# A Fourier mixing and low-rank MLP kernel: batch 1 folded at the output with even and odd products, channel steps of batches 1 and 2 given out by need, one of the first narrow sums on GpSimd

## The chip, the cores and the metric

The kernel runs on one NeuronCore of a Trainium2 chip. The engines are named as in the profile: PE (TensorE, matmuls; PEld are its weight loads), DVE (VectorE), ACT (ScalarE), POOL (GpSimd) and SP (SyncE, which issues DMAs). The metric is the device time of one execution in microseconds. Lower is better.

## The reference

```
X  = fft(fft(x, axis=1), axis=2).real          # x: 8 x 3136 x 256, f32
h  = (X^T @ U @ V)^T                           # U: 3136 x 32, V: 32 x 3136, per batch
u  = X + h
out = u + relu(u @ w_ch1) @ w_ch2              # w_ch1: 256 x 1024, w_ch2: 1024 x 256
```

The real part of a two-dimensional transform of real data is a sum of products with cosine and sine tables: along the sequence (3136 points) and along the channels (256 points). The rest is a low-rank token mixer and a two-layer MLP over channels with a residual.

## The kernel before

All 8 x 3136 rows are cut into 49 chunks of 512 rows. The main loop runs over chunks `c` and, in each, over eight hidden tiles `j`. At each `j` it does `first_product(c, j)` (two matmuls of 512 columns, line 735, and a ReLU on ACT, line 737). At each odd `j` it does `second_product(c - 1, j // 2)` (eight matmuls of 256 columns, line 751); every second one of these is closed by three sums on DVE into the output tile (lines 757, 759, 760). At `j == 3` it calls `front(c + 1)`, which makes the next chunk's input u: two low-rank matmuls (line 709) and sums with the transformed data on DVE (line 725, one for each half of the channels, S and T). The tile u is also transposed by DMA for the output sums.

Between these, the loop runs small steps from a table `due`, keyed by 8 x c + j. They prepare the later batches, b = 1 to 7 (batch 0 is done ahead of the loop; b counts from 0, so "second batch" is b = 1). For each batch there are:

- `fold(b)`: 16 steps that fold x along channels and sequence on DVE (`along_d`, line 386; `mirror`, line 395; `half`, line 399), with the loads of the next batch among them, issued by POOL.
- `seq(b, par, typ, pn)`: the sequence transform, eight steps. A pair of steps gives the products of the even and of the odd tiles (line 485, four matmuls of 425 columns each), which DVE sums into the tiles A and B (lines 500, 504). From batch 2 on the first of a pair is split further into narrower matmuls (`quarters`, line 446); `halves` (line 430) is a form with two groups of 229 columns, used in batch 1 for one of the two types.
- the channel transform. Batches 0 and 1 use `chan`: for each of four column ranges and each half h two matmuls (lines 631, 633) and a copy. From batch 2 on `even_ch` and `odd_ch` use half the matmuls (lines 643, 652): the even product is copied by ACT (line 645), and DVE forms its sum and difference with the odd one (line 654). `across` copies rows of A into the low-rank operand on ACT (lines 664, 666), so that the missing term comes out of the low-rank product.
- `narrow`: channel 0 needs a product of its own, with one row (batches 0 and 1) or six rows (batches 2 to 7 together, `column_steps`), and narrow sums (lines 570 to 574), on DVE for batch 0 and on POOL for the others.
- `joined(b)` (line 468, POOL) joins the sums for U, and from batch 2 on it also sends the first-channel row by DMA on SP's queue (line 673). `lowrank(b)` (line 678) makes the low-rank operand TA (line 680, ACT), which `front` reads.

The order up to chunk 1 is written out by hand. From there a planner orders each engine's instructions, with program order as priority: an instruction that it takes for ready may pass one that it takes for blocked. The fold's instructions are pinned behind what stands ahead of them on their engine. PSUM is shared: three buffers ("dft") for the products of all these steps, three for the first product, two for the second.

For batch b the low-rank step is due at about `hi`:

```
hi = 8 * (b * S // CH - 1) + 2        # 42, 90, 138, 186, 234, 282, 330 for b = 1 to 7
```

## Time and profile before

| what | value |
|---|---|
| median of three runs | 447.18 us (447.13 to 447.69) |
| the profiled execution | 447.31 us |
| its span | 445.2 us |
| granted TensorE clock | 1.00 throughout |
| DVE busy | 353.1 us, 79% |
| ACT busy | 297.5 us, 67% |
| POOL busy | 85.7 us, 19% |

The columns of a row of the profile's timeline are: start and length in us, engine, source line, operation, output <- inputs, shapes, how many were merged, and, in brackets, the idle time before it with what ended it. In the groups the mean is in ns. A matmul's end is modelled and overlaps the next matmul, so the cost of a matmul is read from the start of its neighbour. DVE instructions overlap a little too.

### The profile page before, as it was taken

What the parts mean: (1) busy time and instruction counts of PE and PEld (TensorE: products, weight loads), DVE (VectorE), ACT (ScalarE), POOL (GpSimd) and SP (SyncE); (2) the same over time, 40 slices, a digit from 0 to 9 for tenths busy, and PEclk for the clock granted to TensorE, in tenths of its full rate; (3) what the DMA queues carried; (4) which work ended last, traced back from release to release, by engine and by line L of the source; (5) the groups of instructions that cost most, each with busy time, mean ns of one, the idle gap of its engine ahead of it and who ended that gap; (6) DMA issues with size and microseconds to landing.
All of it is one profiled execution on the core that took longest, in us unless ns stands there. A gap on an engine that the chain in (4) does not pass through costs nothing.

```text
span 445.2 us, 8087 instructions
## 1 busy us (share of the span) xinstructions
PE 435.7 (98%) x2960; PEld 316.4 (71%) x3012; DVE 353.1 (79%) x838; ACT 297.5 (67%) x564; POOL 85.7 (19%) x144
## 2 busy tenths in 40 slices
PE   8999999999999999999999999999999999999997
PEld 6456766776677777777777777777777777777775
DVE  8879998888998799878998789878998776443433
ACT  8857747565885669655875569655876569656562
POOL 8973217300931002300211001300000000000000
PEclk9999999999999999999999999999999999999999
DMA  7998997995199437674779537782333332434343
GB/s 133 210 230 180 229 173 117 245 153 103 49 230 265 120 106 216 190 171 73 157 203 222 108 103 216 196 167 71 95 119 95 91 100 73 117 97 121 93 125 112
DMA packets 103249, 65.36 MB, mean 147 GB/s; under 512 B 73806, under 2 KB 99624, under 8 KB 100464
## 3 DMA queue, kind: packets, MB, share of 16 engines
q1 hardware_dynamic: 97528, 39.10, 40.1%
q0 software_dynamic: 5664, 25.75, 21.6%
q8 instruction: 23, 0.38, 0.3%
q14 instruction: 16, 0.13, 0.1%
q10 hardware_dynamic: 18, 0.00, 0.0%
HBM read 29.33 MB, written 25.69 MB: 124 GB/s over the span
## 4 chain that ended last, share of the span: by engine, by line
PE 91%; DVE 2%; DMA 2%; issue 1%; POOL 1%; ACT 1%; DVEq 0%; POOLq 0%
PE p L751 38%; PE p L735 35%; PE pt L485 6%; PE ph L709 5%; DMA xb<-in_x_dram,xidx 2%; PE ptq L446 2%; PE pst L643 1%; PE pst L652 1%; PE m L850 1%; PE ptc L556 1%; ACT h L737 0%; DVE eor L386 0%; PE pst L631 0%; DVE eof L386 0%; PE pst L633 0%
## 5 line engine op out<-in xcount | busy, mean ns | idle before, releaser
L737 ACT ACTIVATE h<-p 128x512 bf16<-128x512 f32 x392 | 222.0, 597 | 119.5 <-PE p L735 107.3
L735 PE MATMUL p<-u,w 128*128 128x512 bf16 x735 | 209.3, 379 | 1.2 <-DVE B L500 0.2
L751 PE MATMUL p<-w,h 128*128 128x256 bf16 x1568 | 203.0, 273 | 1.4
L751 PEld LDWEIGHTS <-h 128*128 128x128 bf16 x1568 | 153.2, 98 | 50.4 <-DVE o L760 0.3
L735 PEld LDWEIGHTS <-w 128*128 128x128 bf16 x784 | 106.1, 144 | 35.1 <-issue 2.0
L757 DVE TENSOR_TENSOR o<-p,ut 128x4 f32<-128x4 f32 (+1 forms) x100 | 16.2, 162 | 54.9 <-PE p L751 53.3
L759 DVE TENSOR_TENSOR o<-p,ut 128x254 f32<-128x254 f32 (+1 forms) x100 | 40.5, 405 | 0.0
L760 DVE TENSOR_TENSOR o<-p,ut 128x254 f32<-128x254 f32 (+1 forms) x100 | 40.5, 405 | 0.0
L468 POOL TENSOR_TENSOR tab<-tf 128x64 bf16<-128x64 f32 x7 | 3.1, 440 | 179.2 <-DVE tf L492 179.1
L386 DVE TENSOR_TENSOR eof<-xf 99x1024 bf16<-99x1024 f32 x28 | 35.8, 1293 | 0.0
L386 DVE TENSOR_TENSOR eor<-xr 99x1024 bf16<-99x1024 f32 x28 | 34.8, 1247 | 0.0
L725 DVE TENSOR_TENSOR u<-ph,S 128x512 bf16<-128x512 f32 (+23 forms) x63 | 34.3, 553 | 0.0
L725 DVE TENSOR_TENSOR u<-ph,T 128x512 bf16<-128x512 f32 (+23 forms) x63 | 34.2, 553 | 0.0
L55 POOL DMA_INDIRECT xf<-in_x_dram,xidx x14 | 17.3, 1234 | 62.0 <-DVE eof L386 48.5
L709 PE MATMUL ph<-va,ta 128*128 128x512 bf16 (+15 forms) x124 | 28.6, 328 | 0.3
L485 PEld LDWEIGHTS <-g 98*128 98x128 bf16 (+1 forms) x152 | 14.7, 98 | 13.1 <-issue 0.7
L395 DVE TENSOR_TENSOR eos<-eof,eor 99x1024 bf16<-99x1024 bf16 (+1 forms) x28 | 19.2, 702 | 0.0
L654 DVE TENSOR_TENSOR S<-evd,pst 128x392 bf16<-128x392 f32 (+1 forms) x24 | 13.5, 564 | 6.4 <-PE pst L652 4.1
L485 PE MATMUL pt<-tabs,g 98*128 98x425 bf16 x80 | 17.6, 344 | 0.0
L457 DVE TENSOR_TENSOR ev<-ptq,ex 128x131 f32<-128x131 f32 (+1 forms) x24 | 6.9, 289 | 12.9 <-ACT ex L450 12.9
L399 DVE TENSOR_TENSOR g<-eos 99x2048 bf16<-99x2048 bf16 (+1 forms) x14 | 16.9, 1217 | 0.0
L485 PE MATMUL pt<-tabc,g 98*128 98x425 bf16 x72 | 15.5, 344 | 0.0
(198 smaller groups left out, 381.0 us busy)
## 6 DMA issues: line engine op xcount, KB each, us to landing
out_dram<-o SPq DMA_DIRECT2D x48, 512.0 KB
xr<-in_x_dram POOLq DMA_DIRECT2D x14, 784.0 KB, 8.2
xb<-in_x_dram POOLq DMA_DIRECT2D x2, 392.0 KB, 7.9
ut<-u SPq DMA_TRANSPOSE x49
w<-in_moe_w_ch_dram POOLq DMA_DIRECT2D x1, 512.0 KB
out_dram<-o SPq DMA_DIRECT2D x4, 128.0 KB
va<-in_moe_V_dram POOLq DMA_DIRECT2D x2, 196.0 KB
w<-in_moe_w_ch_dram POOLq DMA_DIRECT2D x1, 256.0 KB, 7.2
```

Of the source, the lines that this page charges most:

```text
L55: nc.gpsimd.indirect_dma_start(out_, None, bass.AP(t.tensor, t.offset, [[w, rows], [1, w]]), bass.IndirectOffsetOnAxis(idx, 0), element_of ...
L386: pin(nc.vector.tensor_tensor(dst[:, a, :, part * P:(part + 1) * P].rearrange("p i (k t) -> p i k t", k=2), lo, hi, op=AL.subtract if part ...
L395: pin(nc.vector.tensor_tensor(EOS[:, a, :, cols], EOF_[:, a, :, cols], EOR_[:, a, ::-1][:, :, cols], op=op))
L399: pin(nc.vector.tensor_tensor(G[b % 2][par][:, :, cols], EOS[:, 0, :, cols], EOS[:, 1, :, cols], op=AL.add if par == 0 else AL.subtract))
L485: nc.tensor.matmul(pt[:], g[:kp(i), i, P * typ:P * (typ + 1)], tabs[typ][:kp(i), i, par, :], start=(n == 0), stop=(n == NI // 2 - 1))
L709: nc.tensor.matmul(ph, TA[b % 2][:k, s * P:(s + 1) * P], VA[b % 2][:k, lo:hi], start=start, stop=True)
L725: nc.vector.tensor_tensor(u[:, s, col:col + hi - lo], ph[:, col:col + hi - lo], src, op=AL.add)
L735: nc.tensor.matmul(p1[:], W1[:, s, j::JT], k["u"][:, s, :], start=(s == 0), stop=(s == 1))
L737: LAST[0] = nc.scalar.activation(k["h"][:, j, :], p1[:], AF.Relu)
L751: nc.tensor.matmul(p2[:, t % w, :], h[:, j, rs], W2[:, j, :], start=(j == 0), stop=(j == JT - 1))
L759: nc.vector.tensor_tensor(o[:, ts, 1:P], p2[:, :w, 1:P], ut[:, ts, 1:P], op=AL.add)
L760: nc.vector.tensor_tensor(o[:, ts, P + 1:D], p2[:, :w, P + 1:D], ut[:, tT, P - 1:0:-1], op=AL.add)
```

## The change

1. Batch 1's sequence step uses the split form `halves` for both types, where it used it for one.
2. Batch 1's channel step is `even_ch`, `odd_ch` and `across`, as in the later batches, in place of `chan` with two matmuls for each half. Its low-rank product then reads all 128 rows of the operand, and the separate `last_row` sums of batch 1 are gone.
3. `transform` is cut into `sequence` and `channels`, and each gets its own due times. Channels of batches 1 and 2 come at -4, -3, -2, -1, +3, +5, +8, +11 around `hi`, those of the later batches from -12 to -1. `joined`, the row's DMA (`row_in`) and `lowrank` have due times of their own. The folds of batches 1 and 2 move, the column sums of batches 2 to 7 end five steps earlier, and the column loads are 1.86 steps apart in place of 2.
4. Of the two pairs of narrow sums of batch 0, one goes to POOL. The rows for it are copied to one partition by ACT. `ta_rows(1)` moves ahead of that sum's second half.
5. Batch 1's narrow sums have tiles of their own (`tc1`, `tr1`) and run ahead of the sequence steps.

```diff
-        if pn == 0 and (b >= B0 or b == 1 and typ == 1):
+        if pn == 0 and b:
             (quarters if b >= B0 else halves)(d, g, par, typ)
...
+            if single:
+                odd = t["ev"] = wp.tile([P, QW], FP32, tag="ev", name="evc", bufs=4)
+                nc.scalar.copy(odd[3 * R:3 * R + 1], pt[R:R + 1])
+                t["eo"] = gen.tile([KP, 2, QW], FP32, tag="pho", name="eo")[:1]
+                nc.scalar.copy(t["eo"][:, 0], pt[:1])
+                return
...
+            eng = nc.vector if single and par else nc.gpsimd
+            if single and par == 0:
+                nc.scalar.copy(t["eo"][:, 1], t["pt"][2 * R:2 * R + 1])
+                e, o = t["eo"][:, 0], t["eo"][:, 1]
...
     def joined(b):
         join_t(nc.gpsimd)
-        if b >= B0:
-            nc.gpsimd.tensor_copy(TS[:1, 0], trow[:, (b - B0) * R:(b - B0 + 1) * R])
-            nc.sync.dma_start(out=VA[b % 2][R:R + 1, :], in_=rows[b - B0:b - B0 + 1, :])
+        nc.gpsimd.tensor_copy(TS[:1, 0], trow[:, (b - B0) * R:(b - B0 + 1) * R] if b >= B0
+                              else tr1[:])
+    def row_in(b):
+        nc.sync.dma_start(out=VA[b % 2][R:R + 1, :], in_=rows[b - B0:b - B0 + 1, :])
...
-        k = P if b >= B0 else 2 * R + 1
+        k = P if b else 2 * R + 1
...
-        if b < B0:
-            row = list(first_channel(b, eng=nc.gpsimd))
-            yield from row[:2]
-            yield lambda: (row[2](), joined(b))
-            for ch in range(4):
-                for h in range(2):
-                    yield lambda ch=ch, h=h: chan(b, ch * 392 + (1 if ch else 0),
-                                                  (ch + 1) * 392 + 1, h)
-            yield from row[3:]
-            yield lambda: (lowrank(b), last_row(b))
-            return
+    def channels(b):
         for ch in range(4):
             yield lambda ch=ch: (even_ch(b, ch), across(b, ch, False))
-            yield lambda ch=ch: (odd_ch(b, ch), across(b, ch, True), ch < 3 or joined(b))
-        yield lambda: lowrank(b)
+            yield lambda ch=ch: (odd_ch(b, ch), across(b, ch, True))
...
     narrow_0[0]()
+    narrow_0[2]()
     seq(0, 0, 1, 0)
-    for step in narrow_0[1:3]:
-        step()
+    narrow_0[1]()
+    ta_rows(1)
+    late[1]()
...
-    for step in piece(1, 0) + piece(1, 1, tag=("p2", 2)) + late[2:] + late[:2]:
+    for step in piece(1, 0) + piece(1, 1, tag=("p2", 2)) + late[2:] + late[:1]:
...
         if b == 1:
-            spread(list(fold(b)), 4, 23)
-            spread(list(transform(b)), 23, hi)
+            spread(list(fold(b)), 2, 21)
+            row = list(first_channel(b))
+            spread(row[:1], 21, 22)
+            spread(row[1:], 22, 24)
+            spread(list(sequence(b)), 23, hi - 4)
+        elif b == B0:
+            spread(list(fold(b)), hi - 60, hi - 23)
+            spread(list(sequence(b)), hi - 21, hi - 4)
         else:
             spread(list(fold(b)), hi - 66, hi - 35)
-            spread(list(transform(b)), hi - 33, hi)
+            spread(list(sequence(b)), hi - 33, hi - 13)
         if b == B0:
-            for at, step in zip((24, 23, 21, 20, 19, 18, 12), column_steps()):
+            for at, step in zip((24, 23, 21, 20, 19, 18, 17), column_steps()):
                 due.setdefault(hi - at, []).append(step)
+        due.setdefault(hi - (3 if b <= B0 else 11), []).append(lambda b=b: joined(b))
+        if b >= B0:
+            due.setdefault(hi - 10, []).append(lambda b=b: row_in(b))
+        due.setdefault(hi, []).append(lambda b=b: lowrank(b))
+        at = (-4, -3, -2, -1, 3, 5, 8, 11) if b <= B0 else (-12, -10, -8, -6, -4, -3, -2, -1)
+        for n, step in zip(at, channels(b)):
+            due.setdefault(hi + n, []).append(step)
     for n, step in enumerate(column_loads()):
-        due.setdefault(8 + 2 * n, []).append(step)
+        due.setdefault(8 + 52 * n // 28, []).append(step)
```

More of the change, by code (lines that the diff above doesn't have):

```diff
@@ L517 @@
     trow = cpool.tile([1, NB * R], BF16, name="trow")
+    tc1 = cpool.tile([1, 2, R], FP32, name="tc1")
+    tr1 = cpool.tile([1, R], BF16, name="tr1")
     def column_zeros():
@@ L543, in column_loads, with narrow @@
                     yield load
-    def narrow(nb, stationary, dst, tc_, total, tag=("dft", 3), late=None, eng=None):
+    def narrow(nb, stationary, dst, tc_, total, tag=("dft", 3), single=False, late=None):
         t = {}
-        eng = eng or nc.vector
         def products():
@@ L768, in second_product, with sequence @@
             del CK[c]
-    def transform(b):
+    def sequence(b):
         for par in range(2):
@@ L798, in odd_row @@
     def odd_row(i):
-        pho = gen.tile([KP, 2, NQ], I32, tag="pho", name="pho")
-        phase(pho[:], krow[:KP], ncol[:KP, i:i + 1], 15)
-        sine(tabs[0][:, i, :, :NQ], pho[:], 15, 1)
+        pho = gen.tile([KP, 2, QW], I32, tag="pho", name="pho")[:, :, :NQ]
+        phase(pho, krow[:KP], ncol[:KP, i:i + 1], 15)
+        sine(tabs[0][:, i, :, :NQ], pho, 15, 1)
     odd_row(0)
```

19 lines of the change are left out of this document (9 added, 10 removed).

## The prediction

> **What bounds the kernel now.** I read four views in this order: the busy times on the page, a table of busy time by stage, the timeline of one engine at a time around the places where a chunk of 512 rows begins, and the groups of instructions for prices. A step below is one hidden tile j of one chunk (step = 8·chunk + j), as the kernel's own due times count.
>
> ```profile
> PE 435.7 (98%) x2960; PEld 316.4 (71%) x3012; DVE 353.1 (79%) x838; ACT 297.5 (67%) x564; POOL 85.7 (19%) x144
> ```
>
> ```profile
> 36.00:66.00 30.00, 29.83 (x197) 21.08 (x199) 29.80 (x54) 19.63 (x37) 8.40 (x12) 1.00 0.88 192
> 66.00:76.00 10.00, 9.64 (x68) 6.06 (x68) 8.87 (x16) 7.38 (x16) 6.84 (x8) 1.00 0.75 132
> ...
> 107.00:136.00 29.00, 28.36 (x203) 20.46 (x205) 27.48 (x58) 22.93 (x45) 16.07 (x18) 1.00 0.58 135
> ```
>
> The columns after the length are PE, weight loads, DVE, ACT, POOL, granted clock and DMA. PE idles 445.2 - 435.7 = 9.5 us in the whole span, and in the three stages that the change rearranges only 0.17, 0.36 and 0.64 us. So the time is PE's work plus few stalls. The second engine matters as much: DVE is full from 36 to 66 us (29.80 of 30) and nearly so from 107 to 136. Work that moves from PE to DVE is free only where DVE's queue is not already what a matmul waits for.
>
> **The terms.** Prices of what PE loses, from starts of neighbours, because modelled ends overlap:
>
> ```profile
> 54.62 0.56 PE L430 MATMUL pth<-tabc,g 98*128 98x229 bf16 x4
> 55.02 0.88 PE L485 MATMUL pt<-tabc,g 98*128 98x425 bf16 x4
> 55.74 0.89 PE L485 MATMUL pt<-tabs,g 98*128 98x425 bf16 x4
> ...
> 68.15 0.33 PE L631 MATMUL pst<-A,mc 128*128 128x393 bf16 x1
> ...
> 68.49 0.59 PE L735 MATMUL p<-u,w 128*128 128x512 bf16 x2
> ```
>
> (a) *Second batch, fewer matmuls.* Two more of its sequence products take the split form: four narrow matmuls in 0.40 us (54.62 to 55.02) in place of four wide ones in 0.72 (55.02 to 55.74), 2 x 0.32 = 0.64 us. Its channel step did eight pairs of matmuls at 0.34 us (68.15 to 68.49); the even and odd form does eight single ones, which leaves out 8 x 0.167 = 1.34 us. Together **-1.98 us**, all on PE. Nothing is added on PE: the low-rank product contracts 128 rows in place of 65, but its matmuls of 512 columns start the next one after the same time.
>
> (b) *The first narrow sums, and the fold that begins two steps earlier.* On DVE one of the two pairs of sums goes to POOL, with two more one-row copies on ACT. Where this stage ends is here:
>
> ```profile
> 32.75 1.22 DVE L574 TENSOR_TENSOR va<-evc,ptc 1x392 bf16<-1x392 f32 x2
> 34.09 0.57 DVE L635 CAST T<-pst 128x392 bf16<-128x392 f32 x1
> 34.69 0.69 DVE L725 TENSOR_TENSOR u<-ph,S 128x512 bf16<-128x512 f32 x1
> 35.30 0.68 DVE L725 TENSOR_TENSOR u<-ph,T 128x512 bf16<-128x512 f32 x1
> 35.90 2.35 DVE L386 TENSOR_TENSOR eor<-xr 99x1024 bf16<-99x1024 f32 x2
> ```
>
> ```profile
> 34.46 2.36 PE L735 MATMUL p<-u,w 128*128 128x512 bf16 x10
> ```
>
> Chunk 1's input u is whole at 35.98. A product of 512 columns follows the next after 0.22 us (the row of two at 68.49 takes 0.59, one of three below 0.81), so PE has done the eight matmuls left of chunk 0 at 34.46 + 8 x 0.22 = 36.2 and asks for u: 0.2 us to spare. The change puts the first two folds of batch 1 (together that 2.35) at steps 2 and 3, in program order ahead of the copy at 34.09 and of u. DVE saves one sum there (half of 1.22) and the pause before 34.09 (0.12), so u comes some 2.3 - 0.7 = 1.6 us later. Against that stand the 0.2 to spare, one channel pair that PE can do first (0.34), and that the first half of each product needs only the S half of u, which lands 0.6 us before the T half. I take **+0.6**, between 0 (the planner finds other work) and 1.4. POOL's sums I put at nothing: POOL starts them when ACT has copied the row, and what covers them is the rest of batch 0's sequence on PE; they would show as a wait of the first low-rank products.
>
> DVE's prices for the next parts, from starts of neighbours where there are any:
>
> ```profile
> 45.84 1.23 DVE L386 TENSOR_TENSOR eor<-xr 99x1024 bf16<-99x1024 f32 x1
> 46.98 1.22 DVE L386 TENSOR_TENSOR eof<-xf 99x1024 bf16<-99x1024 f32 x1
> ...
> 56.26 0.35 DVE L436 TENSOR_TENSOR ev<-pth,ev 128x196 f32<-128x196 f32 x1
> ...
> 57.15 0.19 DVE L492 TENSOR_TENSOR tf<-pt,ev 128x32 f32<-128x32 f32 x1
> ...
> 94.73 0.30 DVE L457 TENSOR_TENSOR ev<-ptq,ex 128x131 f32<-128x131 f32 x1 [1.44 <-ACT ex L450]
> ...
> 97.22 0.14 DVE L757 TENSOR_TENSOR o<-p,ut 128x4 f32<-128x4 f32 x1
> ```
>
> ```profile
> L395 DVE TENSOR_TENSOR eos<-eof,eor 99x1024 bf16<-99x1024 bf16 x26 | 17.9, 703 | 0.0
> L399 DVE TENSOR_TENSOR g<-eos 99x2048 bf16<-99x2048 bf16 x12 | 14.6, 1214 | 0.0
> ```
>
> ```profile
> 122.22 0.56 DVE L654 TENSOR_TENSOR S<-evd,pst 128x392 bf16<-128x392 f32 x1
> ...
> 123.16 0.15 DVE L757 TENSOR_TENSOR o<-p,ut 128x4 f32<-128x4 f32 x1
> ...
> 123.89 0.68 DVE L395 TENSOR_TENSOR eos<-eof,eor 99x1024 bf16<-99x1024 bf16 x1
> ```
>
> (c) *Batch 1 is spread out.* Its sequence went into steps 23 to 30, on top of the fold of batch 2 at 24 to 55; now it has 23 to 38, the fold 30 to 67, and its channels 38 to 53. The idle PE time there is the 0.17 + 0.36 above. I take **-0.4** of it, ends 0 and -0.5. DVE gains work here: four odd steps of two sums (0.94 us a pair, 122.22 to 123.16) and two more split products (0.89, 56.26 to 57.15), less one row of sums: at most 4 x 0.94 + 2 x 0.89 = 5.5 us. What hides it is that the fold's tail and batch 2's sequence have left these steps. ACT loses eight copies and gets four, with eight half-height ones, in a stage where it is 65% busy (19.63 of 30).
>
> (d) *Batch 2 is pushed together.* Before, its sequence ran at 57 to 70 and its channels at 72 to 86; now 69 to 83 and 86 to 101, beside the fold of batch 3 at 72 to 101, which stays.
>
> A fold is 8 x 1.14 + 4 x 0.70 + 2 x 1.21 = 14.3 us over 31 steps, 0.46 a step. A sequence is 4 x 2.49 (94.73 to 97.22) = 10.0 us over 17 steps, 0.59. Output and input sums are 2 x 0.73 (123.16 to 123.89) + 2 x 0.61 (34.69 to 35.30) = 2.7 us a chunk, 0.33 a step. From step 72 to 85 that is 1.38 us of DVE a step. PE's chunk is 16 + 2 matmuls of 0.22 and 32 of 0.108 (rows of eight and of twelve below: 0.43 for four), 7.4 us, 0.92 a step, and for the sequence 4 x (0.32 + 0.72) / 17 = 0.25: 1.17. DVE falls behind by 0.21 x 14 = 2.9 us. In the same steps before, its load was 0.33 + 0.46 + 4 x 0.94 / 14 = 1.06 against 1.02, 0.5 us. So DVE is some **2.4 us later** than now when chunks 11 and 12 ask for u. How late it is now:
>
> ```profile
> 119.80 1.04 PE L751 MATMUL p<-w,h 128*128 128x256 bf16 x8
> 120.67 0.82 PE L735 MATMUL p<-u,w 128*128 128x512 bf16 x2
> ```
>
> ```profile
> 120.39 0.68 DVE L725 TENSOR_TENSOR u<-ph,S 128x512 bf16<-128x512 f32 x1
> ...
> 135.77 0.54 DVE L725 TENSOR_TENSOR u<-ph,T 128x384 bf16<-128x384 f32 x1
> ```
>
> ```profile
> 136.56 0.81 PE L735 MATMUL p<-u,w 128*128 128x512 bf16 x3
> ```
>
> Chunk 10's u ends at 121.07, after its first product began at 120.67 (two matmuls took 0.82, elsewhere 0.59): late already. Chunk 12's ends 136.31, 0.25 us before use. With 2.4 us more, u misses by 2.1. The cover is PE's own order, which a planner sets from what it expects to be ready:
>
> ```profile
> 63.21 1.47 PE L751 MATMUL p<-w,h 128*128 128x256 bf16 x12
> ```
>
> Twelve second-product matmuls in a row, where eight is a unit: it moves some ahead when u is late. A chunk has 16 of them ready (1.74 us) at that moment, if buffers are free. So 0.4 us of 2.1 is left, and the stalls from DVE's slowing beside POOL (next) stay. I take **+0.5**, ends -0.6 (the idle there now goes) and +2.1 (nothing is moved ahead). If the cover goes, the next thing late is output sums, then PSUM.
>
> ```profile
> 117.89 1.97 DVE L386 TENSOR_TENSOR eor<-xr 99x1024 bf16<-99x1024 f32 x1
> ```
>
> This fold took 1.97 us in place of 1.23, while POOL did the column sums; the PSUM-fed pair at 122.22 held its 0.56. The Trainium skill, *SBUF — State Buffer*, "Who interferes with whom", says that a VectorE instruction with two SBUF inputs and a GpSimd instruction that reads SBUF shut each other out. The trace agrees (1.97 against 1.23). By that rule POOL's late first sum could hold back the early fold of (b) by up to 0.7 us more, and the sum would be -0.5 in place of -1.2; without it it stays -1.2.
>
> (e) *Batches 3 to 7.* Same work, but the four odd steps come at -10, -6, -3 and -1 before the batch's low-rank step, where they were at -16, -12, -8 and -4: one more pair (0.94 us) just ahead of the next input sum.
>
> ```profile
> 185.69 0.48 DVE L725 TENSOR_TENSOR u<-ph,T 128x320 bf16<-128x320 f32 x1
> ```
>
> ```profile
> 186.60 0.59 PE L735 MATMUL p<-u,w 128*128 128x512 bf16 x2
> ```
>
> u of chunk 18 ends at 186.17, 0.43 us before use; 0.94 later it is 0.5 late, in batches 3 to 6 (behind batch 7 no fold follows). Eight second-product matmuls cover that. I take **+0.1**, ends 0 and 4 x 0.5 = 2.0. The low-rank product goes from two steps ahead to the step itself:
>
> ```profile
> 229.58 0.27 PE L678 MATMUL ptt<-mc,tab 128*128 128x256 bf16 x1
> 230.22 0.35 ACT L680 CAST ta<-ptt 32x256 bf16<-32x256 f32 x1
> ...
> 232.73 0.49 PE L709 MATMUL ph<-va,ta 128*128 128x256 bf16 x3
> ```
>
> Its result is on chip at 230.57, 0.99 us after the matmul's start, and is read 3.15 after it; two steps less (1.85) leave 1.3. It stays covered, by 0.3; taken as 0.
>
> (f) *Queues.* On POOL the join of the sums now stands ahead of the next load of x from batch 3 on; it waits for DVE's last sum at the end of the sequence, four steps or more earlier, and the load has a fold's length to land. On SP the first-channel row is now sent at step 80 of batch 2, and waits for this copy:
>
> ```profile
> 118.84 2.37 POOL L610 COPY rows<-rows 6x1567 bf16<-6x1567 bf16 x1
> ```
>
> It ends at 121.2, and step 80 was 120.67. So SP stands for about half a us; behind it are input transposes that are read a chunk (7.4 us) later. The column loads are only drawn together (28 in 52 steps in place of 56). I put (f) at 0.
>
> **The sum.** -1.98 + 0.6 - 0.4 + 0.5 + 0.1 = -1.2 us. The profiled run took 447.31 us, 2.1 more than its span of 445.2; the sum gives 446.1 for it. Its time is 0.13 above the median of the three runs (447.18), so I predict **446.0 us**, 0.27% less. A change under 0.2% (0.9 us) is about what a measurement of this kernel cannot tell from none.
>
> **Rivals.** *All cover holds.* Spreading batch 1 takes its 0.5 of idle, the planner hides the late u of chunk 1, and the idle 0.6 of stage (d) goes too: -1.98 - 0.5 - 0.6 = -3.1, 444.1 us. For it: DVE's queue is shorter in 36 to 76 us. Against it: the early folds are written by hand ahead of chunk 1's u.
>
> *VectorE's queue becomes the bound (slower).* One mechanism: the input sum u stands in DVE's order behind folds and sequence work, and PE waits at the chunk's first product. Price: 2.1 in (d) in place of my 0.5, and 2.0 in (e) in place of 0.1: -1.2 + 1.6 + 1.9 = +2.3, 449.5 us. For it: chunk 10 is already late at 120.67, and DVE is full. Against it: the run of twelve at 63.21, with DVE full for 30 us and PE idle 0.17. It decides when less than about half of that lateness is filled: from 2.1 us of stalls beyond my terms on the kernel is slower.
>
> *Only the first chunk fails.* u of chunk 1 costs its full 1.4 and stage (d) 1.0: -1.98 + 1.4 - 0.4 + 1.0 + 0.1 = +0.1, 447.3 us, no change.
>
> *The removed matmuls were not the bound (it does not do what it says).* If PE had spare time, 1.98 us less of it would come back as waiting, 447.2 us. Against it: PE idles 0.17 of 30 us in the very stage where most of it goes, and its matmuls follow each other at 0.108 and 0.22 us. The Trainium skill, *Perfetto Trace Analysis*, "Identifying the Most-Contended Engine", warns that matmul busy time is a poor measure and names the busy share of weight loads: here 71%, which would speak for this rival. The start-to-start times do not bear that out, so I leave it a small chance.
>
> **How the numbers follow.** Forecast 0.50, with a range of its own of 445.0 to 446.6 (0.44 of it faster by over 0.2%, 0.06 within), all cover holds 0.12, first chunk fails 0.06, not the bound 0.08, VectorE's queue 0.24. Faster 0.44 + 0.12 = 0.56, same 0.06 + 0.06 + 0.08 = 0.20, slower 0.24. The ends of the terms add up to -3.1 and to +3.5 (1.4 + 0 + 2.1 + 2.0 - 1.98); the range for 8 in 10 goes to the fast case, 444.0, and to the slow one, 449.5.
>
> **What would show each step.** (a) Eight matmuls at the channel line of batch 1, none of the full pairs, and split products only for batch 1; PE busy lower by about 2 us. (b) u of chunk 1 near 37.5 in place of 35.98, and PE's first product of chunk 1 then, with a channel pair ahead of it. (c) PE idle from 52 to 72 us under 0.3, DVE below full there. (d) DVE without a pause from step 72 to beyond 90, u of chunks 11 to 13 ending at or after the first product, and long runs of second-product matmuls; stalls over 2 us there make the forecast wrong to the slow side. (e) 0.3 us or more of PE idle behind each batch's low-rank step would be the same fault, repeated. (f) SP's wait for the row under 1 us. Wrong to the fast side: no stall at 36 us.

## The result and the profile after

The changed kernel takes **453.01 us** (median of four, 452.79 to 453.18), beside 447.15 for the kernel before on the same chip: a ratio of 1.0129, 95% interval 1.0112 to 1.0147. It is 5.9 us slower. Forecast were 446.0 us, range 444.0 to 449.5, so the prediction was wrong in sign and size. In the changed kernel the first product is line 750, the second 766, u 740, the low-rank products 724, the operand's matmul and copy 693 and 695, the channel steps 655 to 678, the ReLU 752.

The busy times of the changed kernel's page, and its table by stage with the columns that the prediction's table has (span 451.1 us):

```profile
PE 439.0 (97%) x3004; PEld 317.6 (70%) x3004; DVE 351.9 (78%) x846; ACT 300.0 (67%) x570; POOL 84.6 (19%) x148
```

```profile
36.00:66.00 30.00, 28.96 (x201) 20.15 (x201) 26.88 (x52) 19.99 (x38) 13.02 (x19) 1.00 0.88 181
66.00:76.00 10.00, 10.00 (x69) 7.22 (x67) 9.97 (x23) 6.24 (x12) 3.29 (x5) 1.00 0.65 143
...
107.00:136.00 29.00, 27.12 (x190) 19.44 (x184) 27.88 (x60) 18.11 (x36) 12.88 (x16) 1.00 0.53 142
```

PE now idles 451.1 - 439.0 = 12.1 us where it idled 9.5. In the three stages of the prediction's table it is 1.04, 0 and 1.88 (before 0.17, 0.36 and 0.64). The busy time of PE has risen although matmuls were taken out, for two reasons that have nothing to do with work. The record of the kernel before lacks 52 of its matmuls (2960, with 3012 weight loads), nearly all of the first product, and the changed kernel's lacks none (3004 of each, eight fewer). Each one that is missing leaves a small hole that reads as idle time: of two kernels below with the same time (the join ahead of the mirror copies, and then the mirror copies late), the one with 52 missing reads 434.2 us busy and the complete one 436.4. So some 2 us of the 9.5, here and in the prediction, are no idle time. And where matmuls no longer follow one another, each modelled end adds to the busy time, so waits have to be read from starts. Three places stand out.

First, the low-rank products, once per batch. These are PE's rows with a wait at line 724 of the changed kernel, for batches 3 to 7, each from the timeline around that batch; the last bracket is the idle time before the row:

```profile
185.19 0.53 PE L724 MATMUL ph<-va,ta 128*128 128x320 bf16 x3 [0.58 <-issue]
...
236.21 0.50 PE L724 MATMUL ph<-va,ta 128*128 128x256 bf16 x3 [0.54 <-issue]
...
287.21 0.48 PE L724 MATMUL ph<-va,ta 128*128 128x192 bf16 x3 [0.53 <-issue]
...
337.93 0.45 PE L724 MATMUL ph<-va,ta 128*128 128x128 bf16 x3 [0.49 <-ACT ta L695]
...
388.64 0.42 PE L724 MATMUL ph<-va,ta 128*128 128x64 bf16 x3 [0.46 <-ACT ta L695]
```

Together 2.60 us. The matmul before each of them is counted to its modelled end, 0.16 us beyond its pitch, so from start to start it is about 5 x 0.16 = 0.8 more, 3.4 us. Batch 1 has the same wait once (79.66 us, 0.63). What the product waits for stands in ScalarE's timeline of batch 3; the operand's second matmul started at 182.95:

```profile
182.61 0.53 ACT L678 COPY va<-A 64x392 bf16<-64x392 bf16 x1
183.15 0.60 ACT L752 ACTIVATE h<-p 128x512 bf16<-128x512 f32 x1
183.76 0.51 ACT L676 COPY va<-A 64x391 bf16<-64x391 bf16 x1
184.29 0.60 ACT L752 ACTIVATE h<-p 128x512 bf16<-128x512 f32 x1
184.79 0.35 ACT L695 CAST ta<-ptt 32x256 bf16<-32x256 f32 x1
```

ScalarE has no pause. The copy of 0.35 us that makes the operand stands behind two channel copies and two ReLUs and starts 1.84 us after its matmul. Before, it was 0.64 (229.58 to 230.22).

Second, chunk 1's first product. DVE and PE of the changed kernel:

```profile
33.33 1.22 DVE L386 TENSOR_TENSOR eor<-xr 99x1024 bf16<-99x1024 f32 x1
34.58 0.57 DVE L647 CAST T<-pst 128x392 bf16<-128x392 f32 x1
35.07 1.22 DVE L386 TENSOR_TENSOR eor<-xr 99x1024 bf16<-99x1024 f32 x1
36.20 0.69 DVE L740 TENSOR_TENSOR u<-ph,S 128x512 bf16<-128x512 f32 x1
36.80 0.68 DVE L740 TENSOR_TENSOR u<-ph,T 128x512 bf16<-128x512 f32 x1
```

```profile
36.94 0.44 PE L750 MATMUL p<-u,w 128*128 128x512 bf16 x1 [0.79 <-DVE u L740]
```

Both folds stand ahead of u, which is whole at 37.48 (35.98 before). The last product of chunk 0 starts at 35.77, so the next one was due at about 35.99 and came 0.95 us late; before, it came at 36.23, on time.

Third, the stage of the third batch. PE, then DVE, then POOL of the changed kernel:

```profile
117.27 0.49 PE L446 MATMUL ptq<-tabc,g 99*128 99x130 bf16 x4 [1.42 <-DVE B L504]
```

```profile
109.90 1.81 DVE L386 TENSOR_TENSOR eof<-xf 99x1024 bf16<-99x1024 f32 x1
...
113.37 2.04 DVE L386 TENSOR_TENSOR eof<-xf 99x1024 bf16<-99x1024 f32 x1
...
116.64 0.58 DVE L504 TENSOR_TENSOR B<-pt,ev 128x392 bf16<-128x392 f32 x1
```

```profile
109.62 1.01 POOL L586 TENSOR_TENSOR rows<-evc,evo 6x392 bf16<-6x392 f32 x1
...
114.39 2.36 POOL L622 COPY rows<-rows 6x1567 bf16<-6x1567 bf16 x1
```

PE stands 1.42 us for one of the three PSUM buffers, which DVE empties late (line 504 ends at 117.22). Two things are ahead of that on DVE: the sequence sums of batch 2 and the folds of batch 3 now fall together, and the folds of 1.2 us take 1.8 to 2.0 while POOL runs the column sums.

### The profile page after: what moved, and what is told of

Same layout as the page of the kernel before. It is cut to its first block, busy times and chain, and to the rows that moved or that the text cites. A ratio compares the mean times of both kernels' runs of the same rounds, so it can differ in the third digit from the quotient of the medians.

```text
span 451.1 us, 8152 instructions
## 1 busy us (share of the span) xinstructions
PE 439.0 (97%) x3004; PEld 317.6 (70%) x3004; DVE 351.9 (78%) x846; ACT 300.0 (67%) x570; POOL 84.6 (19%) x148
## 4 chain that ended last, share of the span: by engine, by line
PE 86%; ACT 5%; DVE 3%; DMA 2%; issue 2%; POOL 1%; DVEq 0%; POOLq 0%; ACTq 0%
PE p L766 35%; PE p L750 35%; PE pt L485 5%; PE ph L724 5%; ACT h L752 2%; DMA xb<-in_x_dram,xidx 2%; PE ptq L446 2%; ACT va L678 1%; PE pst L664 1%; PE m L856 1%; ACT va L676 1%; PE pst L655 1%; PE ptc L557 1%; ACT evd L657 1%; DVE eof L386 0%
## 5 line engine op out<-in xcount | busy, mean ns | idle before, releaser
L752 ACT ACTIVATE h<-p 128x512 bf16<-128x512 f32 x392 | 219.7, 597 | 122.7 <-PE p L750 119.3
L750 PE MATMUL p<-u,w 128*128 128x512 bf16 x784 | 214.3, 380 | 1.2 <-DVE u L740 0.9
L750 PEld LDWEIGHTS <-w 128*128 128x128 bf16 x784 | 107.3, 144 | 37.7 <-DVE u L740 2.2
L724 PE MATMUL ph<-va,ta 128*128 128x512 bf16 (+16 forms) x126 | 30.0, 329 | 3.4 <-ACT ta L695 1.8
L724 PEld LDWEIGHTS <-ta 128*128 128x128 bf16 (+1 forms) x128 | 11.5, 98 | 8.6 <-ACT ta L695 3.1
L666 DVE TENSOR_TENSOR S<-evd,pst 128x392 bf16<-128x392 f32 (+1 forms) x28 | 15.7, 562 | 0.8 <-ACT evd L657 0.5
L450 ACT COPY ex<-ptq 128x360 f32<-128x360 f32 (+1 forms) x24 | 11.0, 456 | 8.1 <-PE ptq L446 4.7
```

The source lines that it names most:

```text
L724: nc.tensor.matmul(ph, TA[b % 2][:k, s * P:(s + 1) * P], VA[b % 2][:k, lo:hi], start=start, stop=True)
L750: nc.tensor.matmul(p1[:], W1[:, s, j::JT], k["u"][:, s, :], start=(s == 0), stop=(s == 1))
L752: LAST[0] = nc.scalar.activation(k["h"][:, j, :], p1[:], AF.Relu)
```

## The experiments

The theory after the result: the loss is made of separate waits, the largest the operand copy behind ScalarE's burst, and TensorE's saving of 1.98 us is real. The rival is the prediction's own slow case, that VectorE's queue makes u late everywhere. The kernel before measured 447.0 to 447.2 us beside all of these runs; ratios are to it. "From the changed kernel" names what an edit starts from.

**Low-rank product two steps earlier** (from the changed kernel).

```diff
-        due.setdefault(hi, []).append(lambda b=b: lowrank(b))
+        due.setdefault(hi - (2 if b > B0 else 0), []).append(lambda b=b: lowrank(b))
```

> The changed kernel (453.0 us), with the low-rank step of batches 3 to 7 two steps earlier, as it was before. Theory 'operand late': ACT's copy of the low-rank operand stands behind a burst of channel copies, and PE waits about 0.7 us for it in each batch (the profile after shows 0.58 us of idle in one row at 185.19). Then 5 x 0.7 = 3.5 us go: 449.5 us. Rival 'VectorE's queue': the loss in these batches comes from the input sum u, late behind channel sums and folds; the low-rank step's place changes nothing, 453.0 us.

Measured 449.96 us, ratio 1.0064 (1.0051 to 1.0077): 3.05 us less by the medians. The groups of the changed kernel and of this one (in us and mean ns, then idle before):

```profile
L724 PE MATMUL ph<-va,ta 128*128 128x512 bf16 (+16 forms) x126 | 30.0, 329 | 3.4 <-ACT ta L695 1.8 <-issue 1.6
```

```profile
L724 PE MATMUL ph<-va,ta 128*128 128x512 bf16 (+16 forms) x126 | 29.1, 328 | 0.8 <-ACT ta L695 0.8
```

The idle time at this line falls from 3.4 to 0.8, what is left being batches 1 and 2. VectorE's 846 instructions come in the same order in both kernels: its queue is not what cost these 3 us.

**Channels spread out again, the low-rank product left at its step** (from the changed kernel).

```diff
-            spread(list(sequence(b)), hi - 33, hi - 13)
+            spread(list(sequence(b)), hi - 33, hi - 18)
...
-        at = (-4, -3, -2, -1, 3, 5, 8, 11) if b <= B0 else (-12, -10, -8, -6, -4, -3, -2, -1)
+        at = (-4, -3, -2, -1, 3, 5, 8, 11) if b <= B0 else (-18, -16, -14, -12, -10, -8, -6, -4)
```

> The changed kernel, with the low-rank step left where the change put it, but the channel steps of batches 3 to 7 spread over -18 to -4 as before (and the sequence ended at -18, which they need). 'Operand late' in its form 'behind the burst': without the burst ACT copies the operand in time, 449.5 us. In its form 'the place alone' (the chain PE, ACT, PE doesn't fit into two steps whatever ACT does): 453.0 us. 'VectorE's queue': u in front of each batch is earlier by one pair of sums, about 0.9 us in batches 3 to 6 where it was late: 450 to 451 us, with the idle at the operand left.

Measured 449.47 us, ratio 1.0064 (1.0045 to 1.0083): 3.5 us less by the medians, as much as the edit above by the ratios, and the same 0.8 us of idle time at line 724. Either edit alone takes the loss away, so it needs both: the late matmul, and the copies that stand ahead of its eviction.

**The same part alone, put into the kernel before.**

```diff
-            yield lambda ch=ch: (odd_ch(b, ch), across(b, ch, True), ch < 3 or joined(b))
+            yield lambda ch=ch: (odd_ch(b, ch), across(b, ch, True),
+                                  ch < 3 or b > B0 or joined(b))
...
-            spread(list(transform(b)), hi - 33, hi)
+            steps = list(transform(b))
+            if b == B0:
+                spread(steps, hi - 33, hi)
+            else:
+                spread(steps[:8], hi - 33, hi - 13)
+                due.setdefault(hi - 11, []).append(lambda b=b: joined(b))
+                for n, step in zip((-12, -10, -8, -6, -4, -3, -2, -1, 0), steps[8:]):
+                    due.setdefault(hi + n, []).append(step)
```

> The kernel before, with one part of the change alone: in batches 3 to 7 the sequence, the channel steps, the join and the low-rank product at the due times of the changed kernel (low-rank product at the step itself, channels drawn together ahead of it). If the late operand behind ScalarE's burst of copies is the steady loss of the change, this part alone brings all of it: 447.1 + 3.5 = 450.6 us (what moving the product back or the channels back gave, 3.1 to 3.5). If the loss there needs the other parts of the change, it stays below 448.1 us.

Measured 451.13 us, ratio 1.0085 (1.0071 to 1.0099): 4.0 us more, and the groups of this kernel show the wait (0.3 in the kernel before):

```profile
L709 PE MATMUL ph<-va,ta 128*128 128x512 bf16 (+16 forms) x126 | 29.9, 329 | 2.7 <-ACT ta L680 2.6
```

Shown from both sides: this part is 3.0 to 4.0 us of the 5.9.

**The first folds two steps later** (from the changed kernel).

```diff
-            spread(list(fold(b)), 2, 21)
+            spread(list(fold(b)), 4, 23)
```

> The changed kernel, with the fold of batch 1 from step 4 as before, and not from step 2. Theory: the two folds ahead of chunk 1's input cost PE about 1.0 us (chunk 1 begins at 36.94 in place of 35.97): 452.0 us. Rival: the wait moves to the next place where DVE is behind, 453.0 us.

Measured 452.43 us, ratio 1.0132 (1.0113 to 1.0151): 0.6 less by the medians and nothing by the ratios (1.0129 for the changed kernel), so the time does not show a gain. The trace shows that the wait is gone: u stands ahead of the folds and PE does not stop (DVE, then PE):

```profile
35.45 0.68 DVE L740 TENSOR_TENSOR u<-ph,T 128x512 bf16<-128x512 f32 x1
36.05 2.35 DVE L386 TENSOR_TENSOR eor<-xr 99x1024 bf16<-99x1024 f32 x2
```

```profile
34.48 2.36 PE L750 MATMUL p<-u,w 128*128 128x512 bf16 x10
```

**Both first narrow sums on VectorE** (from the changed kernel).

```diff
-            eng = nc.vector if single and par else nc.gpsimd
+            eng = nc.vector if single else nc.gpsimd
...
-    narrow_0[2]()
     seq(0, 0, 1, 0)
     narrow_0[1]()
+    narrow_0[2]()
...
```

The one-row copies on ScalarE go with it, and the second half of the sums stands where it did before the change.

> The changed kernel with both of the first narrow sums on VectorE in the old order, the rest as changed. If the late u of chunk 1 comes from the early folds alone, VectorE has one more sum of 0.6 us ahead of it and the time rises by 0.6, to 453.6 us. If GpSimd's slower sum (1.0 us for a row of 392) and the two one-row copies on ScalarE hold the start back, it falls by 0.5, to 452.5 us.

Measured 453.04 us, ratio 1.0126 (1.0111 to 1.0142): neither of the two expected times, and no change. PE's first product of chunk 1 starts at 37.29 us in place of 36.94, so the sum on GpSimd does save VectorE 0.35 us there, and that is not seen in the time. This part of the change is worth nothing measurable.

**Batch 2 at its old due times** (from the changed kernel).

```diff
-            spread(list(fold(b)), hi - 60, hi - 23)
-            spread(list(sequence(b)), hi - 21, hi - 4)
+            spread(list(fold(b)), hi - 66, hi - 35)
+            spread(list(sequence(b)), hi - 33, hi - 18)
...
-        at = (-4, -3, -2, -1, 3, 5, 8, 11) if b <= B0 else (-12, -10, -8, -6, -4, -3, -2, -1)
+        at = ((-4, -3, -2, -1, 3, 5, 8, 11) if b < B0 else (-18, -16, -14, -12, -10, -8, -6, -4) if b == B0
+              else (-12, -10, -8, -6, -4, -3, -2, -1))
```

> The changed kernel, with the fold, sequence and channels of batch 2 at the due times of before. Theory: DVE's queue, with sequence work, the fold of batch 3 and POOL's column sums at once, costs PE about 1.4 us more than before in chunks 9 to 12: 451.6 us. Rival: the losses in that stage are the same wherever the steps stand, as the column sums slow DVE in any case: 453.0 us.

Measured 451.69 us, ratio 1.0105 (1.0091 to 1.012): 1.3 less by the medians, 1.1 by the ratios. The stage's row, with PE at 28.55 of 29 where it was 27.12:

```profile
107.00:136.00 29.00, 28.55 (x206) 20.48 (x205) 27.48 (x58) 22.80 (x44) 15.96 (x18) 1.00 0.57 146
```

The folds beside the column sums are as slow here as they were:

```profile
113.16 3.26 DVE L386 TENSOR_TENSOR eof<-xf 99x1024 bf16<-99x1024 f32 x2
...
118.03 1.98 DVE L386 TENSOR_TENSOR eor<-xr 99x1024 bf16<-99x1024 f32 x1
```

PE's longest wait in the stage is 0.37 us all the same. So the slow folds alone do not make the loss; it takes the sequence of batch 2 falling together with them. Whether it would be there with folds at their plain length is not shown.

**Column sums earlier** (from the changed kernel).

```diff
-            for at, step in zip((24, 23, 21, 20, 19, 18, 17), column_steps()):
+            for at, step in zip((30, 29, 28, 27, 26, 25, 24), column_steps()):
...
-        due.setdefault(8 + 52 * n // 28, []).append(step)
+        due.setdefault(8 + 48 * n // 28, []).append(step)
```

> The changed kernel with the column sums on GpSimd six to seven steps earlier (and their loads drawn together to 48 steps from 52), the rest as changed. If the third batch's 1.3 us come from VectorE's folds being slowed while GpSimd reads beside them (1.8 to 2.0 us in place of 1.2), the loss moves with the column sums to a place with more room and the time falls by 0.5 to 1.0, to 452.2 us. If they come from the order of VectorE's queue alone (fold of batch 3, sequence of batch 2 and channels drawn into the same steps), nothing changes: 453.0 us.

Measured 459.16 us, ratio 1.0261 (1.0247 to 1.0275): 6.2 more, foreseen by neither. The time says nothing on the question, because new waits arose elsewhere (some 4 us around 72, 4 us around 103); how they doubled stands under the last heading. The wait of 1.42 us is not there in this run (PE's named waits from 107 to 136 us add to 0.3), but VectorE stood idle for 2.00 and 2.80 us just before, so that does not separate the two causes either. What it does answer is on DVE: an `eof` fold of the same stage, clear of GpSimd's sums here (they end before it), is at its plain length, 1.21 where the changed kernel has 1.81 and 2.04.

```profile
118.08 1.21 DVE L386 TENSOR_TENSOR eof<-xf 99x1024 bf16<-99x1024 f32 x1
```

The Trainium skill, *SBUF — State Buffer*, "Who interferes with whom", has a VectorE instruction with two SBUF inputs contend with a GpSimd instruction that reads SBUF. The traces agree: 1.21 without, 1.81 and 2.04 beside such reads.

**The folding of batch 1 alone, in the kernel before.**

```diff
-        if pn == 0 and (b >= B0 or b == 1 and typ == 1):
+        if pn == 0 and b:
...
-                for h in range(2):
-                    yield lambda ch=ch, h=h: chan(b, ch * 392 + (1 if ch else 0),
-                                                  (ch + 1) * 392 + 1, h)
+                yield lambda ch=ch: (even_ch(b, ch), across(b, ch, False))
+                yield lambda ch=ch: (odd_ch(b, ch), across(b, ch, True))
```

> The kernel before, with only the folding of batch 1 at the output taken over: its sequence products all in the split form, its channels as even and odd single products with the sums on VectorE, the low-rank product over 128 rows; every due time and the first narrow sums as before. If TensorE's work in batch 1 is what bounds (term (a) of the prediction), it comes out 1.98 us lower, at 445.2 us. If VectorE, which was full from 36 to 66 us in the kernel before and gets up to 5.5 us more in the same steps, is what bounds there, the saving comes back as waiting: 447.2 us, and up to 450.7 (447.2 - 1.98 + 5.5) if nothing covers it.

Measured 448.96 us, ratio 1.004 (1.0027 to 1.0054): 1.9 more than before, so 1.98 saved became 3.9 of waiting. Its table by stage and, below, PE's waits from 60 to 106 us (sum, count, longest):

```profile
36.00:66.00 30.00, 29.83 (x203) 21.55 (x205) 29.83 (x55) 19.00 (x37) 8.40 (x12) 1.00 0.93 189
66.00:76.00 10.00, 8.17 (x56) 4.76 (x56) 10.00 (x22) 7.34 (x15) 6.59 (x8) 1.00 0.62 130
```

```profile
PE p L735 <- ACT h L737: 1.0, 3, 0.6
PE p L751 <- ACT h L737: 0.6, 1, 0.6
PE ph L709 <- ACT evd L645: 0.5, 1, 0.5
```

DVE is full, as the expectation had it, but what PE names is ScalarE: its copies for eight channel steps come in eight loop steps, each ReLU between two of them. At the old due times the folding is a loss.

**All due times back, the folding kept** (from the changed kernel).

```diff
-            spread(list(fold(b)), 2, 21)
+            spread(list(fold(b)), 4, 23)
...
-            spread(list(sequence(b)), 23, hi - 4)
+            spread(list(sequence(b)), 23, hi - 8)
-            spread(list(fold(b)), hi - 60, hi - 23)
-            spread(list(sequence(b)), hi - 21, hi - 4)
+            spread(list(fold(b)), hi - 66, hi - 35)
+            spread(list(sequence(b)), hi - 33, hi - 18)
...
-            spread(list(sequence(b)), hi - 33, hi - 13)
+            spread(list(sequence(b)), hi - 33, hi - 18)
...
-        due.setdefault(hi - (3 if b <= B0 else 11), []).append(lambda b=b: joined(b))
+        due.setdefault(hi - (6 if b < B0 else 4 if b == B0 else 11), []).append(lambda b=b: joined(b))
...
-        due.setdefault(hi, []).append(lambda b=b: lowrank(b))
-        at = (-4, -3, -2, -1, 3, 5, 8, 11) if b <= B0 else (-12, -10, -8, -6, -4, -3, -2, -1)
+        due.setdefault(hi - 2, []).append(lambda b=b: lowrank(b))
+        at = (-7, -5, -3, -1, 3, 5, 8, 11) if b < B0 else (-18, -16, -14, -12, -10, -8, -6, -4)
```

> The changed kernel with all due times moved back together: the first folds of batch 1 two steps later, its channels spread over steps -7 to +11, batch 2 and the channels of batches 3 to 7 at the due times before, the low-rank product two steps ahead. If the losses are separate places, the single gains add up: 453.0 - 3.5 (operand copy) - 0.6 (first folds) - 1.3 (third batch) = 447.6 us. If each place only passes its wait on to the next, less than that is gained: 449 us. If the places also held back TensorE's saving of 1.98, it goes below the kernel before: 445.5 us.

Batch 1 does not go back to where it was: its channels stand at -7 to +11, and the column sums stay as the change has them. Measured 447.91 us, ratio 1.0016 (1.0007 to 1.0025). It gains 5.1, about what the single gains add up to (4.95 by the medians), but it is still no faster than before. Two waits for VectorE, 0.58 and 1.19 us, stand between 62 and 69 us. They are not in the changed kernel, where PE's named waits from 36 to 107 us are 0.9 for u and 0.6 for the operand of batch 1; so they came with this run's own due times. The longer one:

```profile
68.29 0.88 PE L485 MATMUL pt<-tabc,g 98*128 98x425 bf16 x4 [1.19 <-DVE u L740]
```

**The first-channel row of batch 1 behind its sequence** (from the kernel with all due times back).

```diff
-            spread(row[:1], 21, 22)
-            spread(row[1:], 22, 24)
             spread(list(sequence(b)), 23, hi - 8)
+            spread(row[:1], hi - 9, hi - 8)
+            spread(row[1:], hi - 8, hi - 6)
```

> As the kernel with all due times back, but the first-channel row of batch 1 (its products, the two copies on ScalarE and the sums on GpSimd) comes behind the sequence of batch 1, in steps 33 to 36, in place of ahead of it in steps 21 to 24. If the row ahead of the sequence is what holds VectorE up (in that kernel it stood idle for 2.0 us until ScalarE had made two copies of 0.5 us for the row and then one for the sequence, and TensorE then waited 1.8 us for VectorE between 62 and 69 us), the wait goes and the time falls from 447.9 to 446.1 us, below the kernel before. If the wait is only the turn from fold to sequence, and the row's sums slow VectorE's folds wherever they run, it stays at 447.9 us.

Measured 448.11 us, ratio 1.0034 (1.0019 to 1.0049): no gain. The two waits did go, and chunk 5 starts at 74.34 us where it did at 77.68, but then one wait takes it all back (PE, then POOL):

```profile
80.47 0.28 PE L693 MATMUL ptt<-msn,tab 128*128 128x256 bf16 x1 [2.06 <-POOL tab L683]
```

```profile
76.17 3.58 POOL L634 COPY va<-va 1x784 bf16<-1x784 bf16 x2
79.83 0.32 POOL L468 TENSOR_TENSOR tab<-tf 128x64 bf16<-128x64 f32 x1
80.21 0.20 POOL L683 COPY tab<-tr 1x32 bf16<-1x32 bf16 x1
```

The join of the low-rank sums (lines 468, 683) stands on GpSimd behind the mirror copies of the row.

A kernel from the same start with six buffers in place of four for the even products and the rows does not fit into the memory of a partition and has no time, so whether those buffers were part of the two waits stays open.

**The row behind the sequence, nothing else** (from the changed kernel).

```diff
-            spread(row[:1], 21, 22)
-            spread(row[1:], 22, 24)
             spread(list(sequence(b)), 23, hi - 4)
+            spread(row[:1], hi - 6, hi - 5)
+            spread(row[1:], hi - 5, hi - 3)
```

> The changed kernel with only the first-channel row of batch 1 put behind its sequence (steps 36 to 39), the rest as changed. TensorE stood idle for 1.0 us from 36 to 66 us, of which the late u of chunk 1 is 0.95, so if PE's own waits there tell the loss, nothing changes: 453.0 us. If the idle time of VectorE that the row brings (1.3 and 1.1 us before two sums of the sequence) is handed on to the stages behind it, the time falls by 0.5 to 1.5, to 452.0 us.

Measured 458.57 us, ratio 1.0258 (1.0238 to 1.0277): 5.6 more, a miss. It is the same wait for line 683, here 2.98 us long, and TensorE then ran at half its clock (last heading).

**The join ahead of the mirror copies** (from the kernel with the row behind the sequence and all due times back).

```diff
-            spread(row[1:], hi - 8, hi - 6)
+            spread(row[1:3], hi - 8, hi - 6)
+            spread(row[3:], hi - 5, hi - 3)
```

> As the kernel with the row behind the sequence, but the two mirror copies of the row on GpSimd (3.6 us there) come behind the join of the low-rank sums (0.5 us) in place of ahead of it. In that kernel chunk 5 began 2.7 us earlier than in the kernel before, and then TensorE waited 2.1 us for the joined sums, which stood on GpSimd behind the mirror copies. If that wait was the last one in batch 1, the time falls by 2.1, from 448.1 to 446.0 us, below both kernels: TensorE's saving of 1.98 is then free with the right order. If VectorE, full from 36 to 76 us in that kernel, is what the wait only hid, the gain stays below 1 us: 447.2 us or more.

**Then the mirror copies behind the low-rank step** (on top of that).

```diff
-            spread(row[3:], hi - 5, hi - 3)
+            spread(row[3:], hi + 1, hi + 3)
```

> As the kernel with the join ahead of the mirror copies, but the two mirror copies of the row come behind the low-rank step (steps 43 and 44, where they came at 37 to 39). In that kernel one mirror copy still ran between the two halves of the join on GpSimd (0.83 us), and TensorE waited 1.7 us for the join's second half. If GpSimd's queue is the wait, 0.9 of the 1.7 goes: 447.5 - 0.9 = 446.6 us. If GpSimd is slow there only beside VectorE, and something else takes the place of the wait, nothing changes: 447.5 us.

**Then the low-rank product of batch 1 two steps later** (on top of that).

```diff
-        due.setdefault(hi - 2, []).append(lambda b=b: lowrank(b))
+        due.setdefault(hi - (2 if b >= B0 else 0), []).append(lambda b=b: lowrank(b))
```

> As the kernel with the mirror copies behind the low-rank step, and the low-rank product of batch 1 at step 42 in place of 40 (the others stay two steps ahead). Two steps are 1.85 us of TensorE work that can run while GpSimd joins the sums. If the wait for the join was the only thing that took batch 1's saving of 1.98 us back, it goes altogether: 447.5 - 1.7 = 445.8 us, below the kernel before. If the operand is then late for chunk 6, as it was in batches 3 to 7, some of it returns: 446.5 to 447.5 us.

These three measured 447.49 us, ratio 1.0006 (0.9997 to 1.0015), then 447.54, 1.0014 (1.0005 to 1.0023), then 447.47, 1.0003 (0.9994 to 1.0012). The first gains 0.6 of the 2.1 by the medians, the others nothing: GpSimd's order stays the same in all three. Its rows in the second of them:

```profile
77.03 0.83 POOL L634 COPY va<-va 1x784 bf16<-1x784 bf16 x1
77.91 1.10 POOL L683 COPY tab<-tr 1x32 bf16<-1x32 bf16 x1
```

PE waits 1.80 us for the second row, with a mirror copy still ahead of it. Moving due times did not change what the planner made of it.

**The row's sums straight into the joined sums, as in the kernel before** (from the kernel with the mirror copies late; the copy at line 683 is gone for batch 1, and with it the sum of 0.24 us that made its row).

```diff
-                          tc1 if b else TF[:1, 0], tr1[:] if b else None, **kw)
+                          TF[:1, 0], None, **kw)
...
-        nc.gpsimd.tensor_copy(TS[:1, 0], trow[:, (b - B0) * R:(b - B0 + 1) * R] if b >= B0
-                              else tr1[:])
+        if b >= B0:
+            nc.gpsimd.tensor_copy(TS[:1, 0], trow[:, (b - B0) * R:(b - B0 + 1) * R])
```

> As the kernel with the mirror copies last, but the sums of batch 1's first-channel row go straight into the sums that the join reads, as in the kernel before, in place of a row of their own that GpSimd copies in behind the join (1.1 us, with a mirror copy of 0.83 ahead of it). In that kernel TensorE waited 1.8 us for this copy at 79 us, and chunk 5 had begun 3.1 us earlier than in the kernel before. If this copy was what took batch 1's saving back, the wait goes and the time falls by 1.5 to 2.0, to 445.8 us, below both kernels. If VectorE, full from 36 to 76 us, is what the wait only hid, it stays at 447 us or more.

Measured **446.00 us** against 447.00, ratio 0.9977 (0.9968 to 0.9986): faster than both kernels. GpSimd's order in this kernel, and its table by stage:

```profile
75.48 1.21 POOL L468 TENSOR_TENSOR tab<-tf 128x64 bf16<-128x64 f32 x1
76.76 2.60 POOL L634 COPY va<-va 1x784 bf16<-1x784 bf16 x2
```

```profile
66.00:76.00 10.00, 9.81 (x69) 6.38 (x70) 10.00 (x21) 8.60 (x17) 6.88 (x9) 1.00 1.01 207
76.00:106.00 30.00, 29.44 (x203) 21.51 (x205) 27.56 (x69) 20.42 (x42) 6.91 (x7) 1.00 0.79 161
```

The join ends at 76.69, PE's product starts at 76.75 without a wait, and DVE, full from 66 to 76, costs PE 0.19 us there. The saving of batch 1 is real; 1.0 us of the 1.98 is seen in the time.

## Why the prediction was wrong, point by point

- **(a) -1.98.** The mechanism was right; its full size was not seen in any run. With the other losses undone the kernel is 1.0 us faster than before (1.2 by the spans, 445.2 and 444.0). The prediction had PE alone in mind: it priced the channel step's eight single matmuls and not what comes with them, ScalarE's copies and GpSimd's one-row copy. At the old due times the folding cost 3.9 us of waits.
- **(b) +0.6.** Right in mechanism: u at 37.48, forecast near 37.5. PE's first product began at 36.94, on the S half alone. The size was 1.1 (the channel pair behind the first two products starts at 37.75, before at 36.66), because no channel pair was found to fill the gap. Undone, the pair starts at 36.68; the time does not show the gain clearly.
- **(c) -0.4.** Held, apart from (b): of the 1.04 us that PE idled from 36 to 66, two waits for u are 0.95, and from 66 to 76 it idled 0. So the 0.53 of before became 0.09. What no term had is batch 1's own low-rank operand behind it, 0.63 us at 79.66.
- **(d) +0.5, ends -0.6 and +2.1.** In the range, in part by luck: 1.3 by the run that undid it. VectorE did fall behind in this stage, as priced, but not at u: chunk 10 to 13's u cost little, and PE stood for a PSUM buffer that VectorE emptied late, which the prediction had named as the thing after next. The slow fold of 1.97 beside POOL was in the prediction too, with its stalls left as they were; what it adds to the delay stays open.
- **(e) +0.1, the step that failed.** "It stays covered, by 0.3; taken as 0" was said of the low-rank operand. The working moved the product by two steps (1.85 us) but kept the eviction (the copy that empties the operand's PSUM buffer) where it was, 0.99 us behind its matmul, as in the row of before. The same change draws the channel steps' ScalarE copies together in front of that eviction: in batch 3 there are six in the 5.4 us ahead of it where there were three. ScalarE runs in order, so its start slipped from 0.64 to 1.84 us, 1.2 later. Cover of 0.3 less 1.2 is 0.9 us missed per batch, and five batches miss between 0.6 and 0.75 each from start to start, 3.4 us together. The prediction counted what the moved channel steps put on DVE and not what they put on ACT; that ACT was 67% busy hid it. It named the sign ("0.3 us or more of PE idle behind each batch's low-rank step would be the same fault, repeated") but expected u to be the cause.
- **(f) 0.** On POOL it failed in batch 1 once the row was moved, by the copy at line 683; in the change as made, no such wait stands on PE. SP stood 2.3 us for the row, over the 1 us named as a sign, but it was issued at 116.78 and the transpose behind it only at 119.55, so that cost nothing.
- **The rivals.** The time is above the slowest rival (449.5). VectorE's queue, the slow rival at 0.24, had the right sign for another reason: its price in (e) was 1.9 us for u late in batches 3 to 6, and u was not what PE waited for there. That the removed matmuls were not the bound is not borne out: without them, and with the waits gone, the kernel is faster.

The parts undone alone, 3.05 + 0.58 + 1.32 us, make 4.95 of the 5.9 by the medians, of which the 0.58 is within the noise; together they give 5.1. Read from starts, the changed kernel is about this (an estimate): -1.98 (a), +1.1 (b), -0.4 (c), +1.3 (d), +3.4 (e), and 0.8 and 0.35 for the operands of batches 1 and 2, which no term had. That is +4.6 of the 5.9; the rest lies in small waits that were not tested. So batch 1's saving is in the changed kernel, behind larger losses.

## What to carry to other kernels

When steps are moved, write down for each what it puts on every engine, and look at the short copy that empties PSUM for a critical operand: on an in-order engine it costs its own time plus all that was drawn in front of it, however low that engine's busy share is. A saving on the bounding engine shows only when the due times and the queues around it are redone, so test a kernel of several edits one by one and all together. Where a planner makes the order, due times may not change it (three runs here), while leaving out two small instructions did.

## What the runs showed of the hardware

Stalls of TensorE can cost twice. In the kernel with only the row moved, PE stood for 2.98 us up to 84.01. By stretches of 2 us (granted clock third from the end):

```profile
82.00:84.00 2.00, 0.00 (x0) 0.00 (x0) 0.00 (x0) 0.00 (x0) 1.75 (x5) 0.80 0.00 0
84.00:86.00 2.00, 1.99 (x9) 1.12 (x10) 0.01 (x1) 0.36 (x1) 0.43 (x1) 0.50 0.70 147
86.00:88.00 2.00, 2.00 (x7) 0.86 (x6) 2.00 (x5) 1.01 (x3) 0.00 (x0) 0.50 0.67 257
```

The clock was 0.50 up to about 90 us, so some 6 us of work went at half speed: nearly 3 us more on top of the 3 of the wait, together about the 5.6 that this run lost. With the column sums earlier, a stall of 2.46 us did the same (eight second products in 1.91 us in place of 1.04), while the stall of 2.06 with the row behind the sequence did not (granted clock 1.00 on both sides). The Trainium skill, *TensorE: Matmul & The Clock Gate*, "Why this matters for your kernels", advises against idle gaps over about 3 us. The traces agree in kind, but here 2.46 was already enough.

Nor does the longest stall decide alone. In the kernel with the column sums earlier the clock also fell around 73 us, behind two waits of which neither reached 1 us (PE, then stretches of 2 us):

```profile
70.79 0.39 PE L724 MATMUL ph<-va,ta 65*128 65x512 bf16 x1 [0.60 <-DVE A L504]
71.02 0.60 PE L750 MATMUL p<-u,w 128*128 128x512 bf16 x2
72.60 1.08 PE L485 MATMUL pt<-tabs,g 98*128 98x425 bf16 x4 [0.98 <-DVE ev L437]
```

```profile
72.00:74.00 2.00, 1.40 (x5) 0.72 (x7) 1.97 (x6) 0.25 (x1) 1.30 (x1) 0.79 0.70 94
74.00:76.00 2.00, 1.78 (x9) 1.28 (x9) 2.00 (x6) 0.60 (x1) 1.36 (x3) 0.50 0.97 233
```

What decides between these cases was not tested.
